# The second layer's first product in blocks of 1024 tokens with 512-column matmuls, and a pool of tiles for the activations that wait

## The chip, the cores and the metric

The kernel runs on one core of a Trainium2 chip. The metric is device time in microseconds (us), the median of three runs. The trace comes from one further, profiled execution. TensorE (PE) does the matmuls and loads their stationary operands (PEld), VectorE (DVE) and ScalarE (ACT) do the elementwise work, and SyncE (SP) issues every DMA.

## The reference

A chunked attention gives x, 3072 tokens by 512. Two feed-forward layers follow, each of 512 to 2048 to 512:

```python
x = attention(q, k, v, mem_k, mem_v)              # 3072 x 512
h = x @ moe_w_in;   x = prelu(h, alpha) @ moe_w_out    # layer 1
h = x @ moe2_w_in                                     # layer 2, first product
out = mish(h) @ moe2_w_out                            # layer 2, second product
```

## The kernel before

Every fp32 operand is split into a high part and the rest, and each product is three matmuls: high by high, high by rest, rest by high. The last two of layer 1's six 512-token blocks (together "wide") and the whole of layer 2 use a seven-product scheme in place of eight products: both operands are cut into two by two quarters, seven sums of quarters (`a11`, `a12`, `s1` to `s4`, `a22`) are multiplied by seven sums of weights, and sums of the seven results give the four result quarters.

**Layer 2 before.** `pair2` (from L1192) makes the first product for one block `blk` of 512 tokens and one of eight pairs `p` of feature groups. The token halves are 256 wide, so each of its matmuls (L1216) has 256 columns: seven products, each of two contraction steps and three terms. Two products share the one PSUM bank `X`, half a bank each; a product adds to what stands in it, so between products ACT copies the bank out (`keep`, L1224) before the next one may write. DVE then adds (L1227), ACT applies Mish (L1230), and `split` (L1234 ACT, L1236 DVE) makes the seven split operands `gs`, in a ring `gp` of eleven tiles. `gemm2_pair` (from L1283) gives back the second product of that block and pair as 42 parts, each one 256-column matmul (L1299): seven weights by six matmuls, into seven PSUM banks that stay open over the eight pairs. When a block's last pair is done `evac2` (from L1366) empties them with one copy (L250) and seven DVE adds (L1324).

**How PE is filled.** The parts wait in a list, and `take(n)` issues n of them between the products of `pair2`:

```python
        product(0, 0, True)
        product(3, 1, False)
        keep(e1, 2)
        take(11)
        product(4, 0, False)
```

So PE works on the parts of the pair before while ACT empties `X`. The order of all instructions is worked out on the host when the program is built: `add` notes each step with an estimated duration, and `Plan.run` runs through them engine by engine, takes among the ready steps the one that is due first, and writes the order out; each engine then works through its own list in order.

**Where weights and inputs come from.** All seven weight sums of each pair are written to memory during layer 1 (`spill`). For the first product five of the seven (`KEPT`) are loaded once and stay on the chip (`reload_in`, L420); the other two, and all seven of the second product, are loaded each time (`sent`, L429), 256 KB each, through a ring `w` of ten tiles. `load_x` (from L1117) loads a block's tokens (L1141), makes the four sums (L1161) and splits all seven (L1149 ACT, L1151 DVE), three pairs ahead, in two alternating sets of tiles.

**Before layer 2.** `pair1` (L1488) is the first product of the wide blocks. After it come the wide second products (L1583, 512 columns, four parts of three matmuls for each of the feature groups, counted 6 each by `take`): two groups of the last block right away, then fourteen in a loop over `order_b`, whose weights come by `reload1` (L406, 512 KB). Layer 2's first `pair2` begins when at most eight such parts are left.

Of the kernel before, what the change touches and what calls it, by code (L numbers as in the profile page):

```python
# [10 lines left out]
F32 = mybir.dt.float32  # L11
# [25 lines left out]
class Ring:  # L37
# [136 lines left out]
def chunked_attention_moe_moe_kernel(  # L174
# [104 lines left out]
    KEPT, SENT = (0, 3, 4, 2, 5), (6, 1)  # L279
    w2k = dp.tile([P, NPAIR * len(KEPT), 512], F32, name="w2k")  # L280
    w2s = dp.tile([P, NPAIR * len(SENT), 512], F32, name="w2s")
    w2o = dp.tile([P, NPAIR * 7 + 1, 512], F32, name="w2o")
    w2_bufs = {"k": Buf(None), "s": Buf(None), "o": Buf(None)}
# [63 lines left out]
    def spill(side, p, at):  # L347
# [22 lines left out]
        for i in (3, 4, 6, 5, 0, 1, 2) + (7,) * (side == "o" and p == NPAIR - 1):  # L370
# [10 lines left out]
            if side == "o":  # L381
                kind, to, n = "o", w2o, p * 7 + i
            elif i in KEPT:
                kind, to, n = "k", w2k, p * len(KEPT) + KEPT.index(i)
            else:
                kind, to, n = "s", w2s, p * len(SENT) + SENT.index(i)
            add("sp", dma_(P * 2048), lambda z=z, to=to, n=n: nc.sync.dma_start(to[:, n, :], z.t.bitcast(F32)), [z], [(w2_bufs[kind], n)], at=at)
# [14 lines left out]
    def reload1(u):  # L402
# [8 lines left out]
    in_places = (  # L411
        [("i", j) for j in (3, 5, 7, 9, 11)] + [("o", j) for j in range(6)] + [("i", j) for j in (2, 4, 6, 8, 10)]
        + [("i", 0), ("i", 1), ("o", 6), ("o", 7)]
    )
    pieces = {}

    def reload_in(n):
        w = slot(*in_places[n], [P, 1024], F32R)
        add(
            "sp", dma_(P * 4096), lambda: nc.sync.dma_start(w.t.bitcast(F32), w2k[:, 2 * n : 2 * n + 2, :].rearrange("p i f -> p (i f)")),  # L420
            [(w2_bufs["k"], 2 * n), (w2_bufs["k"], 2 * n + 1)], [w],
        )
        for i in range(2):
            p, r = divmod(2 * n + i, len(KEPT))
            pieces[p, KEPT[r]] = w, lambda w=w, i=i: w.t[:, i * 512 : (i + 1) * 512]

    def sent(kind, dram, n):
        w = second["w"].next()
        add("sp", dma_(P * 2048), lambda: nc.sync.dma_start(w.t.bitcast(F32), dram[:, n, :]), [(w2_bufs[kind], n)], [w])  # L429
        return w, lambda: w.t  # L430
# [550 lines left out]
    def open_rest():  # L981
        late = second["late"]

        def places(*tags):
            makes, after = [], []
            for tag, last_ in tags:
                makes += in_halves(tag)
                after += [last_, last_]
            return makes, after

        def of_slots(*which):
            return places(*((f"w{side}{j}", slots[side, j]) for side, j in which))
# [3 lines left out]
        second["of_slots"] = of_slots  # L996
        halves_ = [[lambda m=m, i=i: m[:, i * 512 : (i + 1) * 512] for i in range(2)] for m in gstrip.tiles]
        rawbox = in_halves("raw0")
        makes = halves_[0] + halves_[1] + rawbox + [lambda m=m: m().bitcast(F32R) for m in wfs.makes]
        second["g"] = makes, [None] * 4 + [raw2.last[0]] * 2 + wfs.last  # L1000
        slot_x = {m: [maker(cp, [P, 1024], F32R, f"w{side}{j}") for side, j in w] for m, w in enumerate(XW)}
        tiles_x = {m: [in_halves_of(xmakers[m][z], i) for z in range(2) for i in range(2)] for m in range(2)}
        second["x"] = [tiles_x[m] + slot_x[m] for m in range(2)]

    x_box = {}

    def in_halves_of(make, i):
        def go():
            if make not in x_box:
                x_box[make] = make()  # L1010
            return x_box[make][:, i * 2 * BN : (i + 1) * 2 * BN]

        return go

    XW = ((("o", 13), ("o", 14), ("o", 15)), (("o", 11), ("o", 12), ("i", 15)))
# [92 lines left out]
    XS = ("a11", "s1", "s2", "s4", "s3", "a22", "a12")  # L1108
    x_last = {}

# [6 lines left out]
    def load_x(blk):  # L1117
        t0 = blk * BN
        frm = [b for i, b in yds.items() if BLOCKS[i][0] < t0 + BN and t0 < sum(BLOCKS[i])]
        m = blk % 2  # L1120
        xs = {}
        for i, name in enumerate(XS):
            first = xring.last[m] if i < 4 else slots[XW[m][i - 4]]
            x = Buf(second["x"][m][i], [x_last[m, i]] if (m, i) in x_last else first)
            x_last[m, i] = xs[name] = x
        t0_, t1_, t2_ = (second["e" if blk else "v"].next() for _ in range(3))
        temps = {"a21": t0_, "s1": t1_, "s2": t2_, "s3": t0_, "s4": t2_}

        def low(name):
            return xs[name].t[:, BN:].bitcast(F32)  # L1130

        def src(name):
            return temps[name].t if name in temps else low(name)

        def read(name):
            return temps[name] if name in temps else (xs[name], "l")

        for name, r, n in (("a21", 1, 0), ("a22", 1, 1), ("a11", 0, 0), ("a12", 0, 1)):

            def load(name=name, r=r, n=n):  # L1140
                nc.sync.dma_start(  # L1141
                    src(name).rearrange("p (k t) -> p k t", t=HB), yd[:, 2 * n : 2 * n + 2, t0 + r * HB : t0 + (r + 1) * HB]
                )

            add("sp", dma_(P * BN * 4), load, [(f, kk) for f in frm for kk in (2 * n, 2 * n + 1)], [read(name)])

        def split(name):
            x = xs[name]
            add("act", c_(BN), lambda: nc.scalar.copy(x.t[:, :BN], src(name)), [read(name)], [(x, "h")])  # L1149
            add(  # L1150
                "dve", e_(BN), lambda: nc.vector.tensor_sub(x.t[:, BN:], src(name), x.t[:, :BN].bitcast(F32)),  # L1151
                [read(name), (x, "h")], [(x, "l")],
            )

        for to, a, b, op in (
            ("s1", "a21", "a22", nc.vector.tensor_add), ("s2", "s1", "a11", nc.vector.tensor_sub),
            ("s3", "a11", "a21", nc.vector.tensor_sub), ("s4", "a12", "s2", nc.vector.tensor_sub),
        ):
            if to == "s4":
                split("s2")  # L1160
            add("dve", e_(BN), lambda op=op, to=to, a=a, b=b: op(src(to), src(a), src(b)), [read(a), read(b)], [read(to)])  # L1161
        for name in ("a11", "s1", "s4", "s3", "a22", "a12"):
            split(name)
        return xs

    def open_rings():
        def ring_of(makes, after):
            r = Ring(makes)
            r.last = [list(a) for a in after]
            return r  # L1170

# [630 lines left out]
```

## Time and profile before

| | |
|---|---|
| median of three runs | 1073.59 us (1073.46 to 1074.79) |
| the profiled execution's own time | 1074.0 us |
| its span, first to last instruction | 1072.2 us |
| PE busy | 1064.3 us, 99% of the span |
| PEld, DVE, ACT busy | 957.7 us, 776.3 us, 681.5 us |
| DMA | 269.40 MB, 251 GB/s |
| granted TensorE clock | 1.000 |

The span is 1.8 us shorter than the profiled execution's time. Matmuls are pipelined, so a matmul's listed duration is longer than the time from its start to the next one's start; the chain of waits shows the second.

### The profile page before, as it was taken

To read this page: it belongs to the slowest core of one execution; us is meant where nothing else is said; L and a number is where in the kernel's file an instruction comes from. 1 tells how busy PE (TensorE), PEld (TensorE's weight loads), DVE (VectorE), ACT (ScalarE), POOL (GpSimd) and SP (SyncE) were. 2 spreads that over 40 slices of the span, in tenths; PEclk is the share of its full clock that TensorE was granted. 3 is DMA by queue.
4 is the path that set the end of the run, shared out by engine and by line. 5 is a ranking of instruction groups with operands and counts; after the bars stand their busy time and mean duration, and the time that the engine had idled before them with its cause. 6 is when DMAs were issued, how large, how long until landed. Compare 5 with 4: busy or idle time off the path is not lost.

```text
span 1072.2 us, 24551 instructions
## 1 busy us (share of the span) xinstructions
PE 1064.3 (99%) x9257; PEld 957.7 (89%) x9257; DVE 776.3 (72%) x1701; ACT 681.5 (64%) x1718; POOL 6.7 (1%) x19
## 2 busy tenths in 40 slices
PE   9999999999999999999999999999999999999998
PEld 6888888888888887888888999999999999999998
DVE  6899477778887699999742576766676675685654
ACT  6888546566456546787734666666676676676664
POOL 2000000000000000000000000000000000000000
PEclk9999999999999999999999999999999999999999
DMA  9957773786667665889998988878888888887875
GB/s 312 311 189 230 266 261 123 217 271 213 212 190 253 181 202 188 294 290 312 303 310 314 304 262 271 269 241 258 267 260 255 269 263 253 269 261 235 268 243 160
DMA packets 144997, 269.40 MB, mean 251 GB/s; under 512 B 14448, under 2 KB 45680, under 8 KB 144880
## 3 DMA queue, kind: packets, MB, share of 16 engines
q1 hardware_dynamic: 144880, 267.85, 77.6%
q8 instruction: 73, 1.20, 0.5%
q14 instruction: 44, 0.36, 0.1%
HBM read 216.15 MB, written 51.64 MB: 250 GB/s over the span
## 4 chain that ended last, share of the span: by engine, by line
PE 84%; DVE 8%; DMA 4%; issue 1%; ACT 1%; POOL 1%; SPq 0%; DVEq 0%; ACTq 0%; POOLq 0%
PE bank L1216 22%; PE bank L1299 22%; PE bank L1032 13%; PE bank L1081 12%; PE bank L1583 7%; PE bank L1488 5%; PE bank L798 1%; DVE aT L886 1%; PE bank L732 1%; DMA wo<-in_w_in_dram 1%; DVE wo L378 1%; DVE rstrip L1055 1%; PE bank L1601 1%; DVE gl L1045 1%; DVE wo L369 1%
## 5 line engine op out<-in xcount | busy, mean ns | idle before, releaser
L1224 ACT COPY b<-bank 128x512 f32<-128x512 f32 x192 | 102.4, 533 | 116.4 <-PE bank L1216 113.4
L1032 PE MATMUL bank<-xh,wi 128*128 128x512 f32 (+1 forms) x528 | 170.9, 386 | 0.0
L1081 PE MATMUL bank<-gh,wo 128*128 128x512 f32 x512 | 170.2, 392 | 0.0
L1032 PEld LDWEIGHTS bank<-xh,wi 128*128 128x128 f32 x528 | 98.2, 188 | 19.9
L1081 PEld LDWEIGHTS bank<-gh,wo 128*128 128x128 f32 x512 | 96.1, 188 | 20.6
L1227 DVE TENSOR_TENSOR b<-b,b 128x256 f32<-128x256 f32 x190 | 79.4, 422 | 42.0 <-ACT b L1224 40.0
L1230 ACT ACTIVATE b<-b 128x256 f32<-128x256 f32 x192 | 79.8, 417 | 35.2 <-DVE b L1227 32.6
L1032 PE MATMUL bank<-xl,wi 128*128 128x512 f32 (+1 forms) x264 | 101.1, 383 | 0.0
L1227 DVE TENSOR_TENSOR b<-b 128x256 f32<-128x256 f32 x142 | 59.8, 421 | 55.7 <-ACT b L1224 52.2
L1081 PE MATMUL bank<-gl,wo 128*128 128x512 f32 x256 | 99.7, 390 | 0.0
L1044 ACT CAST gh<-rstrip 128x512 fp32r<-128x512 f32 x64 | 40.5, 632 | 46.9 <-PE bank L1081 26.2
L1051 ACT ACTIVATE rstrip<-bank 128x512 f32<-128x512 f32 x64 | 38.9, 608 | 43.8 <-PE bank L1032 42.8
L1055 DVE SCALAR_TENSOR_TENSOR rstrip<-rstrip,nalpha 128x512 f32<-128x512 f32 x64 | 47.9, 749 | 23.7 <-ACT rstrip L1052 22.9
L1216 PE MATMUL bank<-wo,wi 128*128 128x256 f32 x432 | 61.9, 283 | 0.3 <-ACT b L1224 0.3
L1045 DVE TENSOR_TENSOR gl<-rstrip,gh 128x512 fp32r<-128x512 f32 x64 | 44.1, 689 | 20.0 <-ACT gh L1044 19.3
L1032 PEld LDWEIGHTS bank<-xl,wi 128*128 128x128 f32 x264 | 49.6, 188 | 9.4
L886 DVE STREAM_TRANSPOSE aT<-s 32x256 f32<-32x256 f32 x128 | 55.8, 436 | 2.4
L1216 PEld LDWEIGHTS bank<-wo,wi 128*128 128x128 f32 x432 | 56.3, 192 | 0.7 <-ACT b L1224 0.5
L1081 PEld LDWEIGHTS bank<-gl,wo 128*128 128x128 f32 x256 | 48.1, 188 | 9.7
L751 ACT ACTIVATE s<-bank,su 128x64 f32<-128x64 f32 x160 | 48.9, 354 | 7.4 <-DVE su L768 7.4
L1216 PE MATMUL bank<-xl,wi 128*128 128x256 f32 x360 | 48.9, 283 | 0.0
L1583 PE MATMUL bank<-wi,wo 128*128 128x512 f32 x192 | 47.2, 390 | 0.0
(247 smaller groups left out, 2423.0 us busy)
## 6 DMA issues: line engine op xcount, KB each, us to landing
wi<-w2o SPq DMA_DIRECT2D x201, 256.0 KB, 3.7
wo<-w2o SPq DMA_DIRECT2D x132, 256.0 KB, 3.8
wo<-w1o SPq DMA_DIRECT2D x49, 512.0 KB, 4.2
w2o<-wo SPq DMA_DIRECT2D x57, 256.0 KB, 3.0
wi<-w2s SPq DMA_DIRECT2D x56, 256.0 KB, 3.6
wo<-in_w_out_dram SPq DMA_DIRECT2D x24, 512.0 KB, 7.8
w2k<-wo SPq DMA_DIRECT2D x40, 256.0 KB, 2.9
wo<-w2s SPq DMA_DIRECT2D x40, 256.0 KB, 3.7
```

The source lines that it names most:

```text
L886: nc.vector.transpose(dst[:, :, m // 2, m % 2], src[:, :, keys])
L1032: nc.tensor.matmul(bk.t[:, lo:hi], a, b, start=kk == 0 and i == 0, stop=kk == KT - 1 and i == 2)
L1045: add("dve", d_(n), lambda: nc.vector.tensor_sub(g.t[1], src.t[0], g.t[0].bitcast(F32)), [src, (g, "h")], [(g, "l")], at=at)
L1055: lambda: nc.vector.scalar_tensor_tensor(r.t[0], m.t[0], nalpha[:, j : j + 1], r.t[0], ALU.mult, ALU.add),
L1081: nc.tensor.matmul(bk.t[:, :n], lt, rh, start=j == 0 and i == 0, stop=j == NJ - 1 and i == 2)
L1216: nc.tensor.matmul(X.t[:, half * HB : (half + 1) * HB], l, r, start=start and kk == n == 0, stop=kk == 1 and n == 2, skip_group_check=True,)
L1224: add("act", c_(n * HB), lambda: nc.scalar.copy(e.t[:, : n * HB], X.t[:, : n * HB]), [X], [(e, i) for i in range(n)])
L1227: add("dve", e_(HB), lambda: op(at(to), at(a), at(b)), [v[a], v[b]], [v[to]])
L1230: add("act", c_(HB), lambda: nc.scalar.activation(at(name), at(name), AF.Mish), [], [v[name]])
L1299: nc.tensor.matmul(bk.t[:, s * HB : (s + 1) * HB], g.t[:, zg * HB + s * P : zg * HB + (s + 1) * P], piece()[:, zw * HB : (zw + 1) * HB], s ...
L1488: nc.tensor.matmul(bk.t, l, r, start=start and kk == n == 0, stop=kk == 1 and n == 2, skip_group_check=True,)
L1583: nc.tensor.matmul(bk.t, lt, rh, start=first and i == 0, stop=last_ and i == 2)
```

## The change

`pair2` takes a superblock `sb` of 1024 tokens in place of a block of 512. Its token halves are two whole blocks, so its matmuls have 512 columns and half as many are issued; a product fills a whole bank. `double` (the first four pairs of the first superblock) uses two banks and alternates with two more; all other pairs use bank 3 alone and take 12 parts after each of the seven products. What it makes is the finished activations of two blocks. The earlier block's go into the list `later` at once, the later block's after the eight pairs of the superblock; until then they stay unsplit in tiles of `pool`. `take` turns entries of `later` into parts (`ready`, which calls `operands` for the sums and splits, then `gemm2_pair`) when parts of less than 30 are left. So one `pair2` and two `gemm2_pair` go together, and the second product of the last blocks is issued with no `pair2` beside it.

`pool` starts with 30 tiles of 512 columns, and `grow_pool` adds seven. Weights go through `wpool`, eight tiles; all seven of the first product are now loaded, once for each superblock, and of the second product's seven two are kept for every pair (`keep_out`). `load_x` fetches a superblock's inputs into ten tiles of `pool` after the sixth pair, `split_x` splits them after the eighth, into one set of tiles. `gp` has twelve tiles. The fourteen wide groups (`unit`) also go into `later`, so they mix with the first `pair2`; parts of weight 60, that is ten wide parts, come before it. In `pair1` the fourth tile is only taken from the ring where no other place is set for it.

```diff
+class Pool:
+
+
+    def __init__(self):
+        self.free = []
+
+    def add(self, make, after):
+        self.free.append((make, list(after)))
+
+    def get(self):
+        return Buf(*self.free.pop(0))
+
+    def put(self, b):
+        self.free.append((b.make, [b]))
...
+    w2i = dp.tile([P, NPAIR * 7, 512], F32, name="w2i")
...
+    kept = {}
+
+    def keep_out(p, side, j):
+        w = slot(side, j, [P, 1024], F32R)
         add(
+            "sp", dma_(P * 4096), lambda: nc.sync.dma_start(w.t.bitcast(F32), w2o[:, 7 * p : 7 * p + 2, :].rearrange("p i f -> p (i f)")),
+            [(w2_bufs["o"], 7 * p + i) for i in range(2)], [w],
         )
...
+    def sent(side, n):
+        w = wpool.get()
+        dram = {"i": w2i, "o": w2o}[side]
+        add("sp", dma_(P * 2048), lambda: nc.sync.dma_start(w.t.bitcast(F32), dram[:, n, :]), [(w2_bufs[side], n)], [w])
         return w, lambda: w.t
...
+    pool, wpool = Pool(), Pool()
+    x_ops = {}
...
+    def open_pool():
...
+        for j in range(9, 13):
+            for m in tiles_of(f"wo{j}", 2, F32R):
+                wpool.add(m, slots["o", j])
+        late = second["late"]
+        for i in range(4):
+            for h in range(2):
+                pool.add(second["v"].makes[2 * i + h], second["v"].last[2 * i + h])
+        for h in range(2):
+            pool.add(lambda h=h: late([P, 1024], "b4")()[:, h * BN : (h + 1) * BN], second["tt"].last[0])
+        for tag, n, after in (
+            ("xh1", 4, wide["t"].last[0]), ("xl1", 4, wide["t"].last[1]), ("xh0", 4, xring.last[0]), ("xl0", 4, xring.last[0]),
+            ("raw0", 2, raw2.last[0]), ("wf0", 1, wfs.last[0]), ("wf1", 1, wfs.last[1]),
+        ):
+            for m in tiles_of(tag, n):
+                pool.add(m, after)
+        for name, hl in zip(("a11", "s1", "s2", "s4", "s3", "a22", "a12"), (
+            (("i", 3), ("i", 5)), (("i", 7), ("i", 9)), (("i", 11), ("i", 12)), (("i", 13), ("o", 13)), (("o", 14), ("o", 15)),
+            (("i", 14), ("i", 15)), (("o", 0), ("o", 1)),
+        )):
+            box = []
+
+            def make(hl=hl, box=box):
+                if not box:
+                    box.extend(maker(cp, [P, 1024], F32R, f"w{side}{j}")() for side, j in hl)
+                return box
+
+            x_ops[name] = Buf(make, slots[hl[0]] + slots[hl[1]])
...
+    X_FROM = (("a11", 0, 0), ("a21", 1, 0), ("a22", 1, 2), ("a12", 0, 2))
+
+    def load_x(sb):
+        src = {}
+        for name, b, k0 in X_FROM:
+            blk = 2 * sb + b
+            for kk in range(2):
+                e = src[name, kk] = pool.get()
+                add(
+                    "sp", dma_(P * BN * 4),
+                    lambda e=e, blk=blk, k=k0 + kk: nc.sync.dma_start(e.t, yd[:, k, blk * BN : (blk + 1) * BN]),
+                    [(yds[blk], k0 + kk)], [e],
+                )
+        for kk in range(2):
+            src["s1", kk] = pool.get()
+        return src
...
+    def split_x(src):
...
         def split(name):
             x = xs[name]
+            for kk in range(2):
+                e, cs = at(name, kk), slice(kk * BN, (kk + 1) * BN)
+                add("act", c_(BN), lambda e=e, cs=cs: nc.scalar.copy(x.t[0][:, cs], e.t), [e], [(x, "h", kk)])
+                add(
+                    "dve", e_(BN), lambda e=e, cs=cs: nc.vector.tensor_sub(x.t[1][:, cs], e.t, x.t[0][:, cs].bitcast(F32)),
+                    [e, (x, "h", kk)], [(x, "l", kk)],
+                )
+
+        def two(to, a, b, op):
+            for kk in range(2):
+                o, l, r = (at(name, kk) for name in (to, a, b))
+                add("dve", e_(BN), lambda o=o, l=l, r=r: op(o.t, l.t, r.t), [l, r], [o])
+
+        add_, sub_ = nc.vector.tensor_add, nc.vector.tensor_sub
+        split("a11")
+        two("s1", "a21", "a22", add_)
+        two("s3", "a11", "a21", sub_)
+        two("s2", "s1", "a11", sub_)
+        split("s2")
+        split("s3")
+        split("a22")
+        split("s1")
+        two("s4", "a12", "s2", sub_)
+        split("s4")
+        split("a12")
+        for e in src.values():
+            pool.put(e)
...
-    def pair2(blk, p, xs, take):
-        X = second["X"]
-        e1, e2, e3, e4 = (second["v"].next() for _ in range(4))
+    def pair2(sb, p, xs, take, double):
+        runs = ((3, 2), (1, 0))[p % 2] if double else (3, 3)
+        e1, e2, e3, e4 = (pool.get() for _ in range(4))
...
+        def product(i, bk, start):
+            w, piece = sent("i", p * 7 + i)
+            x = xs[OPERAND[i]]
+            for kk in range(2):
+
+                def go(kk=kk):
+                    wh, wl = (piece()[:, z * HB + kk * P : z * HB + (kk + 1) * P] for z in range(2))
+                    xh, xl = (t[:, kk * BN : (kk + 1) * BN] for t in x.t)
+                    for n, (l, r) in enumerate(((wh, xh), (wh, xl), (wl, xh))):
+                        nc.tensor.matmul(
+                            bk.t, l, r, start=start and kk == n == 0, stop=kk == 1 and n == 2, skip_group_check=True,
+                        )
+
+                add("pe", 3 * 0.227, go, [w, (x, "h", kk), (x, "l", kk)], [bk])
+            wpool.put(w)
+
+        def keep(e, bk):
+            add("act", c_(BN), lambda: nc.scalar.copy(e.t, bk.t), [bk], [e])
+
+        def more(e, bk):
+            add("dve", e_(BN), lambda: nc.vector.tensor_add(e.t, bk.t, e.t), [bk], [e])
+
+        def mish(e, bk=None):
+            src = bk or e
+            add("act", c_(BN), lambda: nc.scalar.activation(e.t, src.t, AF.Mish), [src], [e])
+
+        A = bank(runs[0])
+        if double:
+            B_ = bank(runs[1])
+            product(0, A, True)
+            product(3, B_, True)
+            keep(e1, A)
+            keep(e2, B_)
+            take(TAKE)
+            product(4, A, False)
+            product(2, B_, False)
+            keep(e3, A)
+            more(e3, B_)
+            mish(e3)
+            take(TAKE)
+            product(5, A, False)
+            more(e2, A)
+            mish(e2)
+            take(TAKE)
+            product(6, A, False)
+            product(1, B_, True)
+            more(e1, B_)
+            mish(e1)
+            mish(e4, A)
+            take(TAKE)
+        else:
+            product(0, A, True)
+            keep(e1, A)
+            take(12)
+            product(4, A, False)
+            keep(e3, A)
+            take(12)
+            product(5, A, False)
+            keep(e2, A)
+            take(12)
+            product(6, A, False)
+            mish(e4, A)
+            B_ = bank(runs[1])
+            take(12)
+            product(3, B_, True)
+            more(e2, B_)
+            mish(e2)
+            take(12)
+            product(2, B_, False)
+            more(e3, B_)
+            mish(e3)
+            take(12)
+            product(1, B_, True)
+            more(e1, B_)
+            mish(e1)
+            take(12)
+        return (e1, e3), (e4, e2)
+
+    def operands(blk, p, r0, r1):
         v = {
-            "p1": (e1, 0), "p5": (e1, 1), "u2": (e2, 0), "a12": (e2, 1), "a22": (e3, 0), "a21": (e4, 0), "a11": (e4, 1),
-            "s1": (e1, 1), "s2": (e2, 0), "s3": (e4, 0), "s4": (e2, 1),
+            "a11": (r0, 0), "a21": (r0, 1), "a12": (r1, 0), "a22": (r1, 1),
+            "s1": (r1, 1), "s3": (r0, 1), "s2": (r0, 0), "s4": (r1, 0),
         }
 
...
         plus, minus = nc.vector.tensor_add, nc.vector.tensor_sub
-        product(0, 0, True)
-        product(3, 1, False)
-        keep(e1, 2)
-        take(11)
-        product(4, 0, False)
-        product(2, 1, False)
-        keep(e2, 2)
-        two("a12", "a12", "u2", plus)
-        mish("a12")
-        take(11)
-        product(5, 0, False)
-        keep(e3, 1)
-        two("a22", "a22", "p5", plus)
-        mish("a22")
-        take(9)
-        product(6, 0, False)
-        product(1, 1, True)
-        keep(e4, 2)
-        two("a11", "a11", "p1", plus)
-        mish("a21")
-        mish("a11")
-        take(11)
...
+        pool.put(r0)
+        pool.put(r1)
         return gs
...
-                held[i] = sent("o", w2o, p * 7 + i)
+                held[i] = kept.get((p, i)) or sent("o", p * 7 + i)
...
+            if s == 1 and n == 2 and not ends and (p, i) not in kept:
+                wpool.put(w)
...
+    parts, later = [], []
+    LOW = 30
+    TAKE = 12
+    PURE = 60
+    DOUBLE = 4
 
     def take(n):
+        while n > 0:
+            while later and sum(w for w, _ in parts) < LOW:
+                later.pop(0)()
+            if not parts:
+                return
             w, part = parts.pop(0)
             part()
             n -= w
...
+    open_pool()
+    src = load_x(0)
+    xnext = split_x(src)
+
...
+    def unit(j):
         e = homes.get(j)
         if not e:
+            e = pool.get()
+            add("sp", dma_(P * BN * 4), lambda: nc.sync.dma_start(e.t, rb[:, j, :]), [(rb_buf, j)], [e])
         split_wide(WIDE + 1, j, e)
+        if j not in homes:
+            pool.put(e)
+        elif j % 2 and j < 12:
+            keep_out((j - 1) // 2 + 2, "i", j - 3)
+        parts.extend(wide_parts(WIDE + 1, j, False, j == NJ - 3))
+
+    def ready(blk, p, r):
+        if (blk, p) == (0, 0):
+            open_gp()
+        if (blk, p) == (0, 1):
+            grow_pool()
+        parts.extend(gemm2_pair(blk, p, operands(blk, p, *r)))
+
+    for p in range(4):
+        keep_out(p, "o", 2 + p)
+    later.extend(partial(unit, j) for j in range(NJ - 2))
+    take(PURE)
+    for sb in range(NB // 2):
+        xs, second_ = xnext, []
         for p in range(NPAIR):
+            ra, rb_ = pair2(sb, p, xs, take, sb == 0 and p < DOUBLE)
+            later.append(partial(ready, 2 * sb, p, ra))
+            second_.append(partial(ready, 2 * sb + 1, p, rb_))
+            if p == 5 and sb + 1 < NB // 2:
+                src = load_x(sb + 1)
+        later.extend(second_)
+        if sb + 1 < NB // 2:
+            xnext = split_x(src)
+    take(999)
```

## Rows read from the trace of the kernel before

**Rows 1.** Busy us by stage: PE, PEld, DVE, ACT, POOL, clock, DMA share, GB/s

```profile
531.50:545.00 13.50, 13.50 (x61) 11.16 (x60) 12.99 (x22) 9.91 (x18) 0.00 (x0) 1.00 0.95 320
545.00:560.00 15.00, 15.00 (x67) 12.22 (x66) 3.94 (x6) 3.11 (x5) 0.00 (x0) 1.00 0.90 295
...
587.00:1061.00 474.00, 473.37 (x3940) 472.71 (x3938) 306.32 (x752) 310.05 (x742) 0.00 (x0) 1.00 0.82 260
```

**Rows 2.** The chain that ended last, in order of time: start, length, what

```profile
180.80 2.72 PE bank L1081 x12
...
522.18 2.72 PE bank L1488 x12
...
531.70 28.69 PE bank L1583 x126
...
719.76 1.44 PE bank L1216 x12
...
751.44 1.44 PE bank L1299 x12
...
779.04 1.68 PE bank L1299 x14
```

**Rows 3.** Waits of PE from 587 to 1072: total us, times, longest

```profile
PE bank L1216 <- ACT b L1224: 0.5, 2, 0.3
```

**Rows 4.** Timeline around one of these waits: start, length, engine, line

```profile
687.63 0.69 DVE L1161 TENSOR_TENSOR rstrip<-b,wo 128x512 f32<-128x512 f32 x1 [1.55 <-DMA b<-yd]
...
688.35 0.62 ACT L1149 CAST xh<-rstrip 128x512 fp32r<-128x512 f32 x1 [1.39 <-DVE rstrip L1161]
...
688.88 0.58 ACT L1224 COPY b<-bank 128x512 f32<-128x512 f32 x1
...
689.51 1.69 PE L1216 MATMUL bank<-xh,wo 128*128 128x256 f32 x12 [0.23 <-ACT b L1224]
```

**Rows 5.** An undisturbed turn of the bank, and dense DVE work

```profile
1040.24 0.88 PE L1216 MATMUL bank<-wi,wo 128*128 128x256 f32 x6
...
1041.16 0.59 ACT L1224 COPY b<-bank 128x512 f32<-128x512 f32 x1 [0.92 <-PE bank L1216]
...
1044.11 0.42 DVE L1236 TENSOR_TENSOR gh<-b,gh 128x256 fp32r<-128x256 f32 x1
...
1044.44 0.42 DVE L1227 TENSOR_TENSOR b<-b 128x256 f32<-128x256 f32 x1
```

**Rows 6.** Groups by line (first: 587 to 1061): total us, mean ns, idle before

```profile
L1224 ACT COPY b<-bank 128x512 f32<-128x512 f32 x140 | 82.2, 587 | 93.7 <-PE bank L1216 92.1
...
L1324 DVE TENSOR_TENSOR rstrip<-bank,rstrip 128x512 f32<-128x512 f32 x24 | 16.5, 687 | 3.8 <-PE bank L1299 3.0
L1498 DVE TENSOR_TENSOR b<-bank,b 128x512 f32<-128x512 f32 x24 | 16.3, 681 | 2.9 <-PE bank L1488 2.9
...
L1503 ACT ACTIVATE b<-b 128x512 f32<-128x512 f32 x19 | 12.0, 630 | 0.4
```

**Rows 7.** Weight loads (line 429): us to landing

```profile
wi<-w2o SPq DMA_DIRECT2D x201, 256.0 KB, 3.7
...
DMA to landing us min/median/max: 2.5/3.7/6.4
```

**Rows 8.** Loads of inputs, and the first of them

```profile
wo<-yd SPq DMA_DIRECT2D x9, 256.0 KB, 4.3
...
523.79 0.79 SPq L1141 DMA_DIRECT2D b<-yd  x1
```

**Rows 9.** The last tiles of the last `pair1` split

```profile
535.29 1.15 ACT L1564 CAST wi<-b 128x512 fp32r<-128x512 f32 x2
...
536.37 1.29 DVE L1565 TENSOR_TENSOR wi<-b,wi 128x512 fp32r<-128x512 f32 x2
```

More of the change, by code (lines that the diff above doesn't have):

```diff
@@ L979, in open_second, with tiles_of, make @@
         second["v"].last = [[b] for b in second["whole"][:4] for _ in range(2)]
[L981 to L992, printed above, removed]
+    def tiles_of(tag, n, dtype=F32):
+        whole, box = maker(cp, [P, n * 512], dtype, tag), []
+        def make(i):
+            if not box:
+                box.append(whole())
+            return box[0][:, i * 512 : (i + 1) * 512]
+        return [partial(make, i) for i in range(n)]
@@ L1001, in open_rest @@
[L1001 to L1013, printed above, removed]
@@ new lines, in grow_pool, with open_gp @@
+    def grow_pool():
+        strip = [x[2] for x in rstrip.live]
+        for i in range(3):
+            pool.add(lambda i=i: rstrip.tiles[0][:, i * BN : (i + 1) * BN], strip)
+        for side, j in (("o", 8), ("i", 10)):
+            for m in tiles_of(f"w{side}{j}", 2):
+                pool.add(m, slots[side, j])
+    def open_gp():
+        makes = [lambda m=m, i=i: m[:, i * 512 : (i + 1) * 512] for m in gstrip.tiles for i in range(2)]
+        after = [g4.last[i] for z in range(2) for i in range(2)]
+        for side, j in (("i", 0), ("i", 1), ("o", 6), ("o", 7)):
+            makes += tiles_of(f"w{side}{j}", 2, F32R)
+            after += [g4.last[2 + j] if side == "i" else slots[side, j]] * 2
+        second["gp"] = Ring(makes)
+        second["gp"].last = [list(a) for a in after]
@@ L1115, in c_ @@
         return 0.12 + 0.94e-3 * n
[L1117 to L1120, printed above, removed]
-        xs = {}
[L1122 to L1145, printed above, removed]
@@ L1147, in split, with at @@
+    def split_x(src):
+        xs = {}
+        for name, old in x_ops.items():
+            xs[name] = old if not old.uses else Buf(old.make, [old])
+        x_ops.update(xs)
+        place = {"s3": "a21", "s2": "a11", "s4": "a11"}
+        def at(name, kk):
+            return src[place.get(name, name), kk]
         def split(name):
             x = xs[name]
[L1149 to L1163, printed above, removed]
@@ L1340, in begin_end @@
         acc = accs[1, blk]
-        p1, u2, u3, u4 = (second["e"].next() for _ in range(4))
+        p1, u2, u3, u4 = (pool.get() for _ in range(4))
         add(BOTH, c_(BN), lambda g: copy_on(g, p1.t, acc[0].t), [acc[0]], [p1])
@@ L1367, in evac2 @@
         acc = accs.pop((1, blk))
-        e = [second["e"].next() for _ in range(4)]
+        e = [pool.get() for _ in range(4)]
         add(BOTH, c_(BN), lambda g: copy_on(g, e[0].t, acc[0].t), [acc[0]], [e[0]])
@@ L1381, in evac2 @@
         store(blk, e[0], 0, 1)
+        for b in e:
+            pool.put(b)
     def wide_x():
@@ L1469, in pair1 @@
         A, B_ = (bank(i + p % 2 * 2) for i in (4, 5))
-        e1, e2, e3, e4 = (second["v"].next() for _ in range(4))
+        e1, e2, e3 = (second["v"].next() for _ in range(3))
         def piece(i, z, kk):
@@ L1532, in pair1 @@
         j0, j1 = 2 * p, 2 * p + 1
+        e4 = homes.get(j0) or second["v"].next()
         last_ = p == NPAIR - 1
@@ L1697, in chunked_attention_moe_moe_kernel @@
         take(12)
-        if 0 < p < 6:
-            reload_in(p - 1)
         if p < NPAIR - 1:
```

124 lines of the change are left out of this document (16 added, 108 removed).

## The prediction

> **What bounds the kernel now.** I read the busy times by stage first. In the stretch that holds nearly all of layer 2, from 587 to 1061, PE is busy 473.4 of 474.0 us at a granted clock of 1.00, its upper level of 2.4 GHz, while DVE and ACT are busy about 306 and 310 us and the DMA engines 0.82 of the time [rows 1]. So nothing feeds PE too slowly there; what counts is how many matmuls there are and how far apart they start. The chain of waits gives that distance, because it lists PE's unbroken stretches: twelve 256-column matmuls take 1.44 us both in the first and in the second product, fourteen take 1.68, that is 0.1200 us each; twelve 512-column matmuls take 2.72 us in layer 1 and in the wide first product, 0.2267 each [rows 2]. The listed durations of single matmuls are of no use for this, since they overlap. Third, PE's own waits: from 587 on they come to 0.5 us in two pieces, both on the copy that empties bank `X` [rows 3]. The timeline around one of them shows how that happens: an input arrived late, DVE waited 1.55 us for it, ACT's cast waited for DVE, and the copy stood behind the cast in ACT's list [rows 4].
>
> **The change, part by part.**
>
> *Matmul count.* The first product is 7 products x 6 matmuls x 8 pairs x 6 blocks = 2016 matmuls of 256 columns and becomes 1008 of 512. Two of the first cost 0.2400 us, one of the second 0.2267, so each replaced pair gives back 0.0133 us and all of them 13.4 us. As all of this lies on the chain, it comes off the end in full if PE stays fed. The 512-column price comes from matmuls of the same kind (split fp32 operands, a new weight tile for each matmul), in three other stages, so I expect no scatter here beyond 0.5 us.
>
> Put otherwise, at 2.4 GHz 256 columns are 0.1067 us and 512 are 0.2133, and both rows show 0.0133 us on top: that part is paid per matmul [rows 2]. The Trainium skill ("TensorE: Matmul & The Clock Gate", section "Wait — 56ns, not 53.3ns?") gives about 2.5 ns as the fixed cost of a warm matmul. By that the sum's first term would be 1008 x 2.5 ns = 2.5 us and not 13.4, which speaks against the change; the trace disagrees, with 13.3 ns, and I go by the trace.
>
> *The turn of the bank.* In 20 of the 24 new `pair2` one bank is used for all seven products, so there are 140 turns in which it must be emptied under the cover of 12 parts, 12 x 0.12 = 1.44 us. An undisturbed turn before: six matmuls from 1040.24 are issued by 1040.96, the copy starts at 1041.16, 0.20 later [rows 5]; the copy takes 0.59 [rows 6]; and from the end of a copy at 689.46 to the waiting matmul is 0.05 [rows 4]. That makes 0.84 us. Three of the seven turns are now a DVE add from the bank, 0.69, hence 0.94, and one is a Mish, taken like the 0.63 of another ACT function of the same size, hence 0.88 [rows 6]. The cover leaves 0.50 to 0.60 us. It is lost only if an instruction of over 0.5 us starts just before on the same engine; the longest such (0.69) would cost 0.2 us. Before, 192 turns under 11 or 9 parts cost 0.5 us. I take 0.3 us, bounds 0 and 3.
>
> *ACT and DVE work.* For two blocks and a pair, ACT's four copies per block become three in all and eight Mish of 256 columns become four of 512; DVE's six adds of 256 become three of 512. The 14 splits and eight sums of the second product remain. Both engines were at about 65% and fall a little, so this costs nothing. The inputs' work is unchanged in amount (22 DVE steps of 0.69 us per superblock, 15.2 us) but there is one set of split operands in place of two: each may be overwritten only after its last use in pair 8, and is needed again one pair later, 7 x 1.36 + 84 x 0.12 = 19.6 us minus the product's own 1.36. Over that pair and the next, 14 to 18 of these steps (10 to 12 us) must go in beside about 20 us of other DVE work in some 35 us. That fits; the inputs are fetched two pairs ahead, so the late input of rows 4 should not recur. Nothing for it in the sum; if that cover fails it is in the first rival.
>
> *The start.* After the last wide first product at 531.5 [rows 2] come 2 + 16 + 10 wide parts of three 512-column matmuls, 28 x 0.68 = 19.0 us, so product 0 is due near 550.6. Three of the ten input tiles are those that the last `pair1` still holds: DVE has split them by 537.7 [rows 9], where before the first input load was issued at 523.8 [rows 8]. Behind these three waits on SP's list stand weight loads, which have time. A load lands in 4.3 us [rows 8], so at 542.0. DVE then needs six steps of 0.69 for `a11` and `s1` (546.1), six for `s3` and `s2` (550.3) and four for `s4` (553.0); four or five splits for the wide groups come in between, about 3 us. `s4` is due at 550.6 + 2.72 + 1.36 + 1.36 = 556.0, so it is on the edge. DVE was full (12.99 of 13.50) at that point and nearly idle right after [rows 1]. I take 0.7 us; bounds 0 and 4, the latter if loads take the 6.4 us that some weight loads took [rows 7].
>
> *Weights.* Loads through the ring of tiles fall from 429 to 405 and the kept ones from 20 of 512 KB to 8, so there is less to move than at 260 GB/s before. But eight tiles serve where ten did. In a full pair 17 loads share eight tiles in 19.6 us, so a tile comes round in 9.2 us; less 1.36 of use, 7.8 remain for a load that takes 3.7, at worst 6.4 [rows 7]. Cost nothing.
>
> *The end without `pair2`.* The list holds 14 x 24 = 336 of wide weight and 47 x 42 + 48 = 2022 parts; taken beside `pair2` are 60 + 4 x 48 + 20 x 84 = 1932. So 426 are left, 51 us of pure second product. DVE needs eleven steps per 42 parts; dense steps start 0.33 us apart [rows 5], so 3.7 of 5.04 us. Five weights per 5.04 us are 260 GB/s, where the DMA engines have shown 320 [rows 1], and a tile comes round in 8.1 us. So PE keeps the lead. But block 5's first part needs a bank that `evac2` has just emptied, and no product covers that any more: 0.84 us for the copy, then one bank per add of 0.69 against 0.72 of parts [rows 6]. I take 1.0 us with the short wait that `begin_end` can now cause; bounds 0.8 and 2.
>
> *Sum,* against the profiled execution's own 1074.0 us: 1074.0 - 13.4 + 0.3 + 0.7 + 1.0 = 1062.6. The median of the runs is 0.4 below that execution, so the forecast is 1062.2 us.
>
> **The rivals.**
>
> 1. *Inputs late.* At the start and at the two changes of superblock DVE gets behind with the splits: 4 us and twice 1 us in place of 0.7, so about 1067. For it: DVE's full stretch and the edge above. Against it: DVE was full then too, and PE stayed at 13.50 of 13.50 [rows 1].
> 2. *Eight weight tiles are too few.* If one load in each of the 24 pairs takes a few tenths longer than its tile's time to come round, 24 x 0.3 = 7 us, and 1069.4. For it: the loads' spread to 6.4 us. Against it: 7.3 to 7.8 us of room.
> 3. *The single bank sets the pace* (slower). Every turn in which the bank's reader stands behind one 0.69 us instruction runs to 1.63 us, 0.19 over its cover; in all 140 turns that is 27 us, and 1089. It decides from 0.10 us per turn, as (11.4 + 2.1) / 140. Against it: rows 3, with shorter cover.
> 4. *The count gives nothing.* If the 13.3 ns went with the columns and not with the matmul, the change would save nothing and pay its 2.0 us: 1075.6, no measurable difference. Against it: three stages with 0.2267. By the skill's 2.5 ns, named above, the result would be 1073.1.
>
> **How the numbers follow.** Forecast 0.72; inputs late 0.10; weights 0.06; bank 0.06; nothing 0.04; 0.02 for more gain than 13.4 - 0.8. The range starts at the full gain with no new wait and without the 0.5 us of rows 3, less the 0.4: 1059.7. It reaches up to 1068.0, over the first rival, and leaves out 0.18. A difference of 0.2%, 2.1 us, is about what can be told from no change: faster 0.90 (the forecast, rivals 1 and 2, more gain), same 0.04, slower 0.06.
>
> **What would show it.** Right: 512-column matmuls of the new `pair2` 0.2267 us apart in the chain, PE idle under 3 us from its first product on, and the last 51 us with second-product matmuls 0.1200 apart and one gap near 0.9 us where block 5 begins. Wrong: PE waiting on the bank's copies or adds all through (rival 3), on input splits near 550 to 560 (rival 1), or on weight loads (rival 2), or 512-column matmuls 0.24 us apart (rival 4).

## The result, and the profile after

The changed kernel takes 1062.54 us, the median of all four runs, against 1073.64 us of the kernel before in the same comparison; the ratio is 0.9891 (95% interval 0.9872 to 0.9911). One of the four, of 1292.03 us, ran with the TensorE clock granted at 0.75 and is left out of the ratio; the other three are 1061.56 to 1063.16. The profiled execution took 1061.56 us, with a span of 1059.8. The prediction was 1062.2 us (1059.7 to 1068.0).

Busy times by stage, columns as in [rows 1], show PE without a gap from the start of layer 2 on:

```profile
531.00:545.00 14.00, 14.00 (x63) 11.60 (x62) 13.43 (x22) 12.75 (x25) 0.00 (x0) 1.00 0.93 306
545.00:560.00 15.00, 15.00 (x68) 12.43 (x67) 8.27 (x14) 6.93 (x11) 0.00 (x0) 1.00 0.96 313
...
587.00:1050.00 463.00, 463.00 (x2963) 421.57 (x2962) 294.01 (x672) 229.58 (x524) 0.00 (x0) 1.00 0.79 246
...
1000.00:1040.00 40.00, 40.00 (x330) 39.74 (x329) 31.63 (x83) 20.59 (x54) 0.00 (x0) 1.00 0.81 261
```

From 587 to 1050 ACT is busy 229.6 us with 524 instructions; in the kernel before, the same 463 us had 303.0 us and 726. DVE fell little, from 300.6 to 294.0.

All listed waits of PE in the whole execution, columns as in [rows 3], lie outside layer 2 (L1545 is in `pair1`, L1659 are the filling matmuls at the kernel's start); the wait on the copy of [rows 3] has no successor, neither on L1228 (`keep`) nor on L1231 (`more`). The list of the weight loads' waits (PEld) is empty from 531 on. PE's are:

```profile
PE bank L1659 <- DVE busy L1657: 1.2, 1, 1.2
PE bank L1545 <- DVE b L1555: 0.6, 3, 0.2
PE bank L1659 <- issue: 0.5, 1, 0.5
```

The chain of waits, columns as in [rows 2] (L1545 `pair1`, L1641 the wide parts, L1220 the new first product, L1352 the parts of the second):

```profile
528.66 2.72 PE bank L1545 x12
531.38 19.07 PE bank L1641 x84
550.45 2.72 PE bank L1220 x12
...
990.28 1.39 PE bank L1220 x6
991.67 1.43 PE bank L1352 x12
993.10 1.39 PE bank L1220 x6
994.49 1.43 PE bank L1352 x12
...
1002.95 50.41 PE bank L1352 x420
```

Three things are to be seen. In the chain the first new product starts at 550.45, where 550.6 was forecast. Twelve 512-column matmuls among others of their width take 2.72 us, as in [rows 2]; but six between two runs of 256-column parts take 1.39 and not 1.36, and the twelve parts after them 1.43 and not 1.44, so that a turn lasts 2.82 us in place of 2.80. And the last 420 parts, with the change from block 4 to block 5 in them, are one unbroken piece of 0.1200 us each.

The groups of the instructions that empty the bank, from 587 to 1061, columns as in [rows 6] (the add, the Mish of what was added, and the copy), have the durations that were taken from before:

```profile
L1231 DVE TENSOR_TENSOR b<-bank,b 128x512 f32<-128x512 f32 x20 | 13.8, 692 | 10.8 <-PE bank L1220 10.2
L1235 ACT ACTIVATE b<-b 128x512 f32<-128x512 f32 x20 | 12.6, 630 | 6.7 <-DVE b L1231 6.7
L1228 ACT COPY b<-bank 128x512 f32<-128x512 f32 x20 | 11.7, 586 | 22.7 <-PE bank L1220 21.5 <-DMA wo<-w2o 1.1
```

The weight loads of layer 2, columns as in [rows 7], land a little sooner than before:

```profile
wo<-w2o SPq DMA_DIRECT2D x237, 256.0 KB, 3.5
wo<-w2i SPq DMA_DIRECT2D x168, 256.0 KB, 3.5
```

The start times of the single matmuls, taken from the trace, say the same as the chain more finely. Distances in ns from each of six such matmuls to the next start, then from the first two parts behind them; in the 133 runs of six no distance differs from these by more than 1:

```
233 236 228 233 230 227 | 113 119 or 120
```

Against 226.7 and 120 that is 20.7 ns more per run, 2.75 us in 133 runs. From the last `pair1` matmul on, no distance is more than 10 ns above 226.7 or 120, so PE waits nowhere there.

### The profile page after: what moved, and what is told of

Its sections match the earlier page's. It is cut to its first block, busy times and chain, and to the rows that moved or that the text cites. A ratio compares the mean times of both kernels' runs of the same rounds, so it can differ in the third digit from the quotient of the medians.

```text
span 1059.8 us, 22415 instructions
## 1 busy us (share of the span) xinstructions
PE 1053.2 (99%) x8249; PEld 905.1 (85%) x8249; DVE 768.2 (72%) x1624; ACT 606.4 (57%) x1507; POOL 6.8 (1%) x19
## 4 chain that ended last, share of the span: by engine, by line
PE 94%; DVE 5%; issue 1%; DVEq 0%
PE bank L1352 23%; PE bank L1220 22%; PE bank L1062 17%; PE bank L1111 17%; PE bank L1641 6%; PE bank L1545 4%; PE bank L803 2%; PE bank L737 1%; PE bank L1659 1%; DVE b L1555 1%; DVE b L1563 1%; DVE wo L392 1%; DVE b L1516 1%; PE bank L614 0%; PE bank L681 0%
## 5 line engine op out<-in xcount | busy, mean ns | idle before, releaser
L1220 PE MATMUL bank<-wi,wo 128*128 128x512 f32 x672 | 180.7, 392 | 0.0
L1220 PEld LDWEIGHTS bank<-wi,wo 128*128 128x128 f32 x672 | 121.5, 189 | 21.3
L1220 PE MATMUL bank<-wo,wo 128*128 128x512 f32 x336 | 93.0, 393 | 0.0
L1352 PE MATMUL bank<-wo,wi 128*128 128x256 f32 x588 | 80.2, 283 | 0.0
L1352 PEld LDWEIGHTS bank<-wo,wi 128*128 128x128 f32 x588 | 77.1, 191 | 3.0
L1352 PE MATMUL bank<-wo,wo 128*128 128x256 f32 x558 | 76.8, 283 | 0.0
L1352 PEld LDWEIGHTS bank<-wo,wo 128*128 128x128 f32 x558 | 73.8, 191 | 3.1
L1220 PEld LDWEIGHTS bank<-wo,wo 128*128 128x128 f32 x336 | 60.8, 189 | 10.1
```

Of the source, the lines that this page charges most:

```text
L1220: nc.tensor.matmul(bk.t, l, r, start=start and kk == n == 0, stop=kk == 1 and n == 2, skip_group_check=True,)
L1352: nc.tensor.matmul(bk.t[:, s * HB : (s + 1) * HB], g.t[:, zg * HB + s * P : zg * HB + (s + 1) * P], piece()[:, zw * HB : (zw + 1) * HB], s ...
```

## The experiments

Each starts from the changed kernel unless it is said otherwise. "The PE stretch" is the time from the start of the last matmul of `pair1` to the start of the last matmul of the kernel: 536.65 us before, 524.23 after.

**The changed kernel once more**, unaltered.

> The changed kernel once more, unaltered, beside the kernel before on the same chip. Theory (matmul count): 13.4 us from 1008 matmuls fewer at 13.3 ns each, 1.4 us from the kernel before's three waits on the bank, less 2.8 us for 133 changes between 256 and 512 columns at 20.7 ns: about 12 us less than before, some 1061.6 to 1062.5. The rival (less work for ACT, DVE and DMA) expects the same time; this run only sets the scale.

1061.56 us (1060.96 to 1062.34), ratio 0.9889 (0.9874 to 0.9904); the kernel before took 1073.75 in the same comparison. The PE stretch is 524.20, so a difference of a few tenths in it can be read.

**The count alone undone.** Each 512-column matmul becomes two of 256 columns with the same operands; ACT, DVE, the DMAs and the order stay those of the changed kernel.

```diff
-                        nc.tensor.matmul(
-                            bk.t, l, r, start=start and kk == n == 0, stop=kk == 1 and n == 2, skip_group_check=True,
-                        )
+                        for h in range(2):
+                            cs = slice(h * HB, (h + 1) * HB)
+                            nc.tensor.matmul(
+                                bk.t[:, cs], l, r[:, cs], start=start and kk == n == h == 0,
+                                stop=kk == 1 and n == 2, skip_group_check=True,
+                            )
...
-                add("pe", 3 * 0.227, go, [w, (x, "h", kk), (x, "l", kk)], [bk])
+                add("pe", 6 * 0.1193, go, [w, (x, "h", kk), (x, "l", kk)], [bk])
```

> The changed kernel with each 512-column matmul of layer 2's first product cut into two of 256 columns, one after the other on the two halves of the bank; all ACT, DVE and DMA work, all tiles and the order around them stay. Theory (matmul count): 1008 more matmuls at 13.3 ns are 13.4 us back, and the 2.8 us for changing between widths go away, so 10.6 us more than the changed kernel, about 1072.5. Rival (the gain comes from less ACT, DVE and DMA work or fewer waits): no more than 1 us above the changed kernel.

1072.74 us (1072.35 to 1075.09), ratio to the kernel before 0.9991 (0.9980 to 1.0003). The PE stretch is 535.44, 11.2 longer than after and 1.2 shorter than before. In the chain (L1355 the parts, L1222 the halved first product) all twelves take 1.44 us again:

```profile
633.94 1.44 PE bank L1355 x12
635.38 1.44 PE bank L1222 x12
636.82 1.44 PE bank L1355 x12
```

So practically the whole gain is in the number of matmuls; what ACT, DVE and the DMAs save is worth the 1.2 us at most. Each matmul here has a weight load of its own, and the run doubles both (1008 to 2016), so the 13.3 ns belong to the two together; no run divides them. The 11.2 agree with 13.4 for the count less what the mixed widths cost in the changed kernel: 2.75, less some 0.5 that stay in the halved kernel where 512-column wide parts mix with 256-column products. The Trainium skill ("TensorE: Matmul & The Clock Gate", section "Wait — 56ns, not 53.3ns?") puts the fixed cost of a warm matmul near 2.5 ns; by that these 1008 matmuls would have cost 2.5 us, which the run excludes.

**Shorter runs.** Two parts are put between the two contraction steps of a product, so that runs of six become runs of three and the width changes more often.

```diff
+                if not double and kk == 0:
+                    take(2)
...
-            take(12)
+            take(10)
```

(the second in all seven places that follow a product of the single bank)

> The changed kernel with two of the twelve parts that follow a product moved into its middle, between the two contraction steps: runs of three 512-column matmuls in place of six, twice as many changes between widths, the same matmuls in all. If every change costs its 20.7 ns: 133 to 140 more of them, 2.8 us more. If the cost sits in the gaps of the run itself (233, 236 ns, then an ordinary last gap, and 113 ns after it): about 9 ns for each of twice as many changes, 2.5 us in all in place of 2.8, so no difference over 0.5 us.

1061.50 us, one run; PE stretch +0.17. The chain (L1354 the parts):

```profile
800.30 1.19 PE bank L1354 x10
801.49 0.69 PE bank L1220 x3
802.19 0.24 PE bank L1354 x2
802.43 0.69 PE bank L1220 x3
```

By the start times, 200 runs of three and 35 of six now stand between parts, in place of 133 of six: 102 changes to the wide kind more, not quite twice as many. A run of three costs 8 ns extra on the mean, a run of six 20 as before. So the cost does not go with the number of changes, by which 2.1 us more were due; the mixed widths cost 0.4 us less than in the changed kernel. That doesn't show in the time, since seven parts between 1017 and 1020 start late by 0.64 us in all, one of them behind a split of the second product (DVE L1311). What in PE the cost comes from stays open.

**Uneven cover.** `take` of 6, 18, 6, 18, 6, 18, 12 in place of seven times 12, to bring the cover below the turn of the bank.

```diff
-            take(12)
+            take(6)
...
-            take(12)
+            take(18)
```

> The changed kernel with 6, 18, 6, 18, 6, 18, 12 parts after the seven products of a pair that uses one bank, in place of 12 each: the same work, but three of the seven turns of the bank have only 0.72 us of cover as written. By the turn worked out in the prediction (0.84 us for a copy, 0.94 for an add) literally applied, two copies and one add fall short by 0.12, 0.12 and 0.22 us in each of 20 pairs: 9.2 us more. Theory (the host's ordering moves the next ready part forward while the bank is not ready): no change beyond 1 us, with 7 or 8 parts found where 6 were written.

1061.88 us, one run, PE stretch unchanged. The edit didn't do what it was meant to: in the trace 9 to 11 parts stand where 6 were written (7 or 8 were expected), because the order worked out on the host brought parts forward into the short places. The next run takes this away.

**Uneven cover, kept.** The same, with `keep` and `more` planned at 0.05 us, so that the host no longer sees the turn.

```diff
-            add("act", c_(BN), lambda: nc.scalar.copy(e.t, bk.t), [bk], [e])
+            add("act", 0.05, lambda: nc.scalar.copy(e.t, bk.t), [bk], [e])
...
-            add("dve", e_(BN), lambda: nc.vector.tensor_add(e.t, bk.t, e.t), [bk], [e])
+            add("dve", 0.05, lambda: nc.vector.tensor_add(e.t, bk.t, e.t), [bk], [e])
```

> The same 6, 18, 6, 18, 6, 18, 12 parts, and the host's ordering is told that the copies and adds that empty the bank take 0.05 us, so that it sees no reason to move parts forward. Theory: PE really waits now, for 0.12, 0.12 and 0.22 us in each of 20 pairs, 9.2 us in all, which measures the turn of the bank at 0.84 and 0.94 us. If the turn is shorter than 0.72 us there is no wait. More than 15 us would mean that the copies and adds also stand behind other work, as in rival 3 of the prediction.

1078.61 us, one run; PE stretch +17.2. The chain now has turns with six parts in front of the product:

```profile
813.98 1.20 PE bank L1352 x10
815.18 1.39 PE bank L1220 x6
816.57 0.71 PE bank L1352 x6
817.28 1.62 PE bank L1220 x6
818.90 2.16 PE bank L1352 x18
821.06 1.39 PE bank L1220 x6
822.45 0.71 PE bank L1352 x6
823.16 1.62 PE bank L1220 x6
824.78 2.16 PE bank L1352 x18
```

The timeline of one of them, columns as in [rows 4]:

```profile
816.41 0.87 PE L1352 MATMUL bank<-wo,wi 128*128 128x256 f32 x6
...
816.61 0.59 ACT L1228 COPY wf<-bank 128x512 f32<-128x512 f32 x1 [0.86 <-PE bank L1220]
...
817.25 1.23 PEld L1220 LDWEIGHTS bank<-wi,wo 128*128 128x128 f32 x6 [0.17 <-ACT wf L1228]
```

The copy starts 0.20 us after the product's last matmul gave way (816.41), takes 0.59, and the next product's weights follow 0.05 later. From 818.90 to 824.78 are 5.88 us, against 5.64 for two turns of 2.82: the short one costs 0.24 more. The matmuls' start times divide it: 246 ns from the last part to the product in place of 120, and then 335 ns to the product's second matmul in place of 233. The first is the turn that was predicted: 0.838 us from the first part (816.408) to the product (817.246); where an add empties the bank the 246 are 354, so 0.946 (predicted: 0.84 and 0.94). The second, 0.10 us each time, was not: a wait of PE on its bank costs more than its own length. The three waits of the kernel before show it too, with 222 or 223 ns behind them in place of 120. Forty short turns with a copy and twenty with an add give 40 x 0.23 + 20 x 0.34 = 16.0 of the 17.2 us, where the turn by itself gave the 9.2 that were expected. The expectation put anything over 15 us down to copies and adds that stand behind other work; the start times speak against that: of 59 late starts that they show only one is later than the turn makes it.

**Four and six weight tiles** in place of eight (`range(9, 11)` and `range(9, 12)`).

```diff
-        for j in range(9, 13):
+        for j in range(9, 11):
             for m in tiles_of(f"wo{j}", 2, F32R):
                 wpool.add(m, slots["o", j])
```

> The changed kernel with four weight tiles in place of eight. Theory (the weight loads are hidden with room to spare): a tile's cycle is about 0.98 us of use, 3.5 to land and 0.3 to issue, 4.8 us; 17 loads on four tiles take 20.4 us against 19.6 of PE work in a full pair, and five loads 5.6 us against 5.04 in the pure second product: 16 us in 20 pairs and 5 us at the end, about 20 us more than the changed kernel. If loads were near their limit with eight tiles already, the loss would be far larger, 50 us and more; if the loads' time hardly mattered, under 5 us.

> The changed kernel with six weight tiles in place of eight. Theory: 17 cycles of 4.8 us on six tiles are 13.6 us against 19.6, so nothing changes (within 0.5 us). By rival 2 of the prediction (eight tiles are already few) 5 us or more are lost.

Four tiles: 1099.00 us; six: 1067.86 (one run each). The PE stretch is 35.1 us longer with four, where 20 were expected, and 5.7 with six, where at most 0.5 were (5 or more by rival 2): both losses were forecast too low. The costliest of PE's waits from 531 on, first with four:

```profile
PE bank L1352 <- DMA wo<-w2o: 7.1, 16, 1.0
PE bank L1220 <- DMA wo<-w2i: 5.6, 8, 1.6
```

and with six:

```profile
PE bank L1220 <- DMA wo<-w2i: 2.2, 4, 0.8
PE bank L1352 <- DMA wo<-w2o: 1.2, 1, 1.2
PE bank L1220 <- DVE b L1303: 0.4, 1, 0.4
```

One of the waits with six tiles, the load and the matmul that waited for it:

```profile
884.54 0.32 SPq L434 DMA_DIRECT2D wo<-w2i  x1
...
889.57 0.70 PE L1220 MATMUL bank<-wi,wo 128*128 128x512 f32 x2 [0.81 <-DMA wo<-w2i]
```

By the start times PE has six long waits on loads with six tiles (the list puts one of them down to DVE). Each of these loads was issued 0.02 us after PE had read the tile's old content for the last time (884.52 here), so nothing held it back in SP's list; it landed 4.4 to 4.9 us later (889.44 here), and PE wanted it after 4.1 to 4.2, in the last case after 3.7. So the prediction's room was too generous in its average: it spread 17 loads evenly over a pair. Where none of the two kept weights is used, each turn of 2.82 us takes three loads, so six tiles last two turns, and 5.64 less the load's own 1.39 us of use leave 4.25. By the same working, an estimate, eight tiles leave 6.1 us beside `pair2` and 5.0 after it, where the slowest load of the changed kernel took 5.2. Eight are enough, since PE has no wait on a load with them, but the margin is less than two tiles.

**The kernel before with earlier inputs**, to see what its own waits on the bank came from. First the inputs are only asked for one pair sooner (from the kernel before):

```diff
-            if p == 2 and blk + 1 < NB:
+            if p == 1 and blk + 1 < NB:
```

> The kernel before with the next block's inputs loaded after the second pair in place of the third. Theory: its three waits on the bank come from late inputs that hold ACT's copy back; earlier loads remove them, 1.4 us less on PE from the end of the wide first product to the last matmul, about 1072.6 us. If the waits have another cause they stay.

1074.69 us, one run; the PE stretch is 536.57, and there are still three waits, with distances of 316, 622 and 374 ns. But the loads had not moved: the host sorts them by when they are due, and they were issued 0.7 to 1.3 us later than before, in a run that is 0.8 us later at the last `pair1`. The wait near 689 us is gone nevertheless; its load took 4.4 us to land and not 5.3. The edit did not do what it was meant to. So, besides, the loads were made due at once:

```diff
-            add("sp", dma_(P * BN * 4), load, [(f, kk) for f in frm for kk in (2 * n, 2 * n + 1)], [read(name)])
+            add("sp", dma_(P * BN * 4), load, [(f, kk) for f in frm for kk in (2 * n, 2 * n + 1)], [read(name)], at=plan.now if blk else None)
```

> The kernel before, with the inputs of the next block asked for after the second pair and made due at once, so that three of the first block's four loads stand earlier in SP's list; all the work is as before. Theory (the three waits of the kernel before, start-to-start gaps of 407, 553 and 504 ns after 120 ns matmuls near 627, 665 and 689 us, come from inputs that land late): the casts find their inputs, the gaps fall to 120 ns, and the distance from the last first product of the wide blocks to the last matmul falls by about 1.1 us, from 536.65 to 535.5. Rival (the 512-column casts stand just ahead of the copy in ACT's list whenever the inputs land): the gaps stay within 0.3 us in sum. If the earlier loads hold back weight loads on the DMA engines, new waits on weights appear in PE's list.

1073.27 us, one run (before: 1073.37); the PE stretch is 536.08, 0.57 shorter where 1.1 was expected. The four loads for the first wait now stand before 600 us (610.54 to 623.28 before), and the one for the third is issued at 676.90: both waits are gone. The second remains, with a distance of 674 ns. Its two loads were issued at 658.29 and 660.46, as before (658.69, 660.85); the products of the block before read their tiles until 656.6. Its timeline:

```profile
663.40 0.62 ACT L1149 CAST wo<-wo 128x512 fp32r<-128x512 f32 x1 [0.68 <-DMA wo<-yd]
...
664.78 0.62 ACT L1149 CAST wo<-wo 128x512 fp32r<-128x512 f32 x1 [0.44 <-DMA wo<-yd]
...
665.31 0.36 ACT L1224 COPY b<-bank 128x256 f32<-128x256 f32 x1
...
665.72 0.98 PE L1216 MATMUL bank<-wo,wi 128*128 128x256 f32 x6 [0.40 <-ACT b L1224]
```

Where the inputs came sooner the wait went, and where they could not it stayed, behind casts that waited for them. That supports the reading of [rows 4]. The second wait grew from 553 to 674 ns, and a new gap of about 0.2 us among the wide parts near 560 us took back some more.

## Why the prediction was right

The total was met to within 0.7 us (1061.56 and 1062.54 for 1062.2). Its largest step was right, and the smaller ones were wrong in ways that cancelled, which was luck.

- **Matmul count, -13.4 us.** Right, by the halved kernel: 11.2 with the cost of mixed widths in it, and the 1.44 and 2.72 us of the chain unchanged where widths don't mix.
- **"so I expect no scatter here beyond 0.5 us"** This step failed. The 512-column price came from three stages in which all matmuls have 512 columns; among 256-column parts six take 1.39 us and not 1.36. It costs 2.75 us and was not in the sum. No row of before showed such a run of layer 2's products.
- **Turn of the bank, +0.3.** The turn itself was sized right (0.838 and 0.946 measured for 0.84 and 0.94), but under 1.44 us of cover it cost nothing, and the waits of before went too. Their start distances of 407, 553 and 504 ns make 1.1 us over 120 each, and the 0.10 behind each of them brings it to 1.4, where the list of [rows 3] had 0.5. The list of the weight loads' waits has all three:

```profile
PEld bank L1216 <- ACT b L1224: 1.2, 3, 0.5
```

  So this term was -1.4 and not +0.3.
- **The start, +0.7.** Came out at nothing: the last of the 14 splits of the first superblock starts on DVE at 550.00 and ends at 550.68, so the one of `s4`, due at 556.0, had over 5 us to spare. The eight loads were not all behind the last `pair1`: the first was issued at 499.4, seven by 535.4, and only the last at 539.94. It landed at 544.1, later than the 542.0 of the prediction, but half of the splits had started by then. DVE (L1177 is `split` in `split_x`, L1623 a wide split):

```profile
549.39 0.69 DVE L1177 TENSOR_TENSOR wi<-b,wi 128x512 fp32r<-128x512 f32 x1
550.00 0.68 DVE L1177 TENSOR_TENSOR wo<-b,wo 128x512 fp32r<-128x512 f32 x1
550.60 1.28 DVE L1623 TENSOR_TENSOR wi<-wi,wi 128x512 fp32r<-128x512 f32 x2
```

- **The end, +1.0.** Nothing, by the unbroken 420 parts. The step took block 5's first part to stand behind the copy. But `evac2`'s copy reads only one bank, which in the order of the last pair is full five weights, 30 parts, before the block ends. So the gap near 0.9 us that was named as a sign did not come. The timeline of the change of blocks (L266 the copy, L1379 the adds):

```profile
1010.70 0.88 PE L1352 MATMUL bank<-wo,wo 128*128 128x256 f32 x6
1010.90 0.59 ACT L266 COPY wo<-bank 128x512 f32<-128x512 f32 x1 [0.43 <-PE bank L1352]
...
1011.52 0.69 DVE L1379 TENSOR_TENSOR xh<-bank,wo 128x512 f32<-128x512 f32 x1
...
1014.30 2.32 PE L1352 MATMUL bank<-wo,wi 128*128 128x256 f32 x18
```

  The copy starts at 1010.90; 30 parts after 1010.70 is 1014.30, when block 5 begins, and the add that frees its first bank ended 2.1 us before, at 1012.21. The other adds keep ahead of the parts in the same way.
- **ACT, DVE and weights at nothing.** Right, as PE waits for none of them; for the weights with less room than the 7.3 to 7.8 us that were worked out, 5.0 to 6.1 by the estimate above.

In the sum: -13.4 for the count, -1.4 for the waits of before and +2.75 for the mixed widths make -12.1; the PE stretch became 12.4 shorter. The rest lies in the kernel before too: two single late starts (at 557.41 and 624.80) of 0.08 us each, and 0.2 us among its wide parts. The terms of 2.0 us that were forecast and did not come stood in for the 2.75 that did.

**The rivals.** Late inputs: no, with 5 us to spare at the start. Too few weight tiles: not with eight, but 6 us with six. The bank sets the pace: only when the cover falls below the turn, and then dearer than worked out from the turn alone, 0.23 to 0.34 us for 0.12 to 0.22. The count gives nothing: excluded by the halved kernel.

## What to carry to other kernels

When PE is busy all the time, count its matmuls and take the distance between their starts from the chain of waits; a wider moving operand gives back the fixed share of each matmul, with its weight load, that is saved, here 13.3 ns. Take that distance from a stretch with the same mix of widths, or keep a few ns per matmul as an uncertainty. Before a wait is charged at the end of an accumulation, look which of its banks the first reader needs and when that one is full. Work out a ring's room for the stretch that uses its tiles fastest, not for the average; and before an experiment with the order is believed, see in the trace that the order did change.

## What the runs showed of the hardware that was not expected

- 512-column matmuls among 256-column ones start up to 236 ns apart and not 226.7, and from the first 256-column one after them to the next start are 113 and not 120 ns; in the changed kernel the pattern repeats to within 1 ns.
- After a wait of PE on its bank the second matmul starts 335 ns after the first and not 233 (222 and not 120 for 256 columns in the kernel before): such a wait cost 0.10 us more than it lasted.
- The list of PE's waits alone undercounts: three waits of 1.1 us between starts appeared there as two of 0.5 us, and under PEld as three of 1.2 us.
